# Values of a sparse attention on 64-column stationary tiles, in a fused attention and maxout kernel

## The chip, the cores and the metric

The kernel runs on one core of one Trainium2 chip. The metric is device time of one execution in microseconds (us). A core has TensorE for matmuls (PE in the profile; its weight loads have a row of their own, PEld), VectorE (DVE), ScalarE (ACT), GpSimd (POOL) and SyncE (SP), which issues most DMAs. A matmul takes a stationary operand (`lhsT`, loaded by an instruction of its own, LDWEIGHTS) and a moving one (`rhs`, streamed through), contracts over the partitions and writes into PSUM, on as many rows as `lhsT` has columns.

## The reference

Attention over q, k, v of shape 4 x 8 x 768 x 64 in fp32, then a maxout layer on the 3072 x 512 result. Each query sees the keys nearer than 16 positions, and 24 block summaries (block of 32: the maximum of the keys, the mean of the values), whose scores are raised by log 32:

```python
k_sum = k.reshape(B, H, nb, block, D).max(axis=3)
v_sum = v.reshape(B, H, nb, block, D).mean(axis=3)
scores_l = scale * np.matmul(q, k.transpose(0, 1, 3, 2))
mask_l = np.abs(pos[:, None] - pos[None, :]) < window
scores_s = scale * np.einsum('bhsd,bhnd->bhsn', q, k_sum) + np.log(block)
scores_all = np.concatenate([np.where(mask_l, scores_l, -1e9), scores_s], axis=-1)
a = softmax(scores_all)                       # over local keys and summaries
attn = np.matmul(a, np.concatenate([v, v_sum], axis=2))
x = attn.transpose(0, 2, 1, 3).reshape(B * S, H * D)
out = np.maximum(x @ w1, x @ w2) @ w_out
```

## The kernel before

**Tiling.** Queries go in 12 tiles of 64 per head. For each tile 128 rows of keys suffice: its neighbourhood and the 24 summaries, which lie among them in rows that the neighbourhood leaves free. So the scores of a query tile are one matmul of 128 keys by 64 queries (`scores`, L566). Two heads go together: head dimension 64 is the contraction, so the two heads' matmuls use rows 0 to 63 and 64 to 127 of the array, as pairs. ScalarE takes the exponential (L591) into tiles `pba` (the first eight query tiles) and `pbb` (the last four), VectorE masks them (L598; in the first batch a matmul adds the mask instead). A `pb` tile has shape 128 x 8 (or 4) x 192: for each head of the pair and each two query tiles it holds 64 columns of the even tile, 64 columns of zeros, and 64 columns of the odd tile. The zeros are set once at the start (`fixed_parts`), and exponential and mask write around them.

**Values.** `values` (L601 to L647) takes one batch, two head pairs (four heads) and one of three groups of four query tiles, 24 calls in all. Each call issues 16 matmuls (`mm`, L609 to L616) into two PSUM banks, one bank per head pair: for each pair of query tiles the even one has stationary columns 0 to 127 of the 192 (even tile, zeros) and the odd one columns 64 to 191 (zeros, odd tile). The moving operand is the values of that tile's 128 key rows with a column of ones (65 columns). The two accumulate, so that the even tile's results end on PSUM rows 0 to 63 and the odd one's on rows 64 to 127. Then VectorE takes the reciprocal of the sums (L625) and multiplies (L627) over all 128 rows, and the result x is transposed, by DMA (L632) or by TensorE (L640).

**Maxout.** x goes through the layer in groups of 256 tokens: w2 - w1 (`wd`) and a product w1 @ w_out (`w1o`, L707) are made once, so that the output is x @ w1o + relu(x @ wd) @ w_out: `hidden` (L723), relu on ScalarE (L728), and the output in `out_part` (L744, L751), copied out of PSUM at L456.

**Order.** A planner (`Plan.run`) sets the order of every engine when the program is made: each operation has an engine, an estimated time and a priority; the planner steps through time, starts on each engine the first ready operation of highest priority, keeps PSUM banks and SBUF buffers in rings, and then issues everything in the order found. The estimate for `values` is 0.48 us. On the chip each engine takes its instructions in that order, with semaphores between engines. Forty small matmul pairs on zeros (`idle`, L785) fill TensorE at the start. The first batch's attention comes early; the other batches' attention lies between the maxout work of the batch before, and the last 29 us are maxout alone.

Of the kernel before, what the change touches and what calls it, by code (L numbers as in the profile page):

```python
# [80 lines left out]
class Task:  # L81
    done, start = 1e9, None
# [29 lines left out]
class Plan:  # L112
# [9 lines left out]
    def op(self, engine, us, fn, read=(), write=(), change=(), touch=(), behind=(), prio=0.0, label="", port=False):  # L122
        t = Task()
        t.engine, t.us, t.fn, t.label = engine, us, fn, label
        t.port = engine == "POOL" or port and engine == "DVE"
        t.prio = (prio + CFG["bump"].get(label, 0), len(self.tasks))
        t.new, t.behind = [*write, *change], behind
        t.deps = {w for b in (*read, *change) for w in b.writers}
        for b in t.new:
            b.writers.append(t)  # L130
        for b in (*read, *touch, *t.new):
            b.users.append(t)
        self.tasks.append(t)
        return t
# [57 lines left out]
def kernel(  # L192
# [14 lines left out]
    nc = tc.nc  # L207
# [23 lines left out]
    def bank(buf, n=512, dt=F32):  # L231
        a = bank_tile[:, buf.slot:buf.slot + buf.width].rearrange("p b n -> p (b n)")
        return (a if dt is F32 else a.bitcast(BF16))[:, 0:n]
# [217 lines left out]
    def copy(engine, us, aps, label, port=True, **kw):  # L451
        engine = ENG[engine]
        us = us if isinstance(us, float) else us[engine[0]]
        def fn():
            o, i = aps()
            {"DVE": nc.vector.tensor_copy, "ACT": nc.scalar.copy,  # L456
             "POOL": nc.gpsimd.tensor_copy}[engine](out=o, in_=i)
        op(engine, us, fn, label=label, port=port, **kw)
# [142 lines left out]
    def values(b, hp, grp, pbs, prio, xt_on="D"):  # L601

        ps, tag = Buf(banks, "av", 2), f"{b}{hp}{grp}"

        def av(h=slice(0, 2)):
            return bank(ps, 1024).rearrange("p (h c) -> p h c", h=2)[:, h, 0:4 * (D + 1)].rearrange(
                "p h (n d) -> p h n d", d=D + 1)

        def mm(h):  # L609
            for n in range(4):  # L610
                u, a = n // 2, n % 2
                pairs = pbs[h][1].ap[:, 2 * a + u] if grp == 2 else pbs[h][0].ap[:, 4 * a + 2 * grp + u]
                for par in range(2):
                    nc.tensor.matmul(out=av()[:, h, n, :], lhsT=pairs[:, 64 * par:64 * par + 128],  # L614
                                     rhs=vx[b].ap[:, 4 * grp + 2 * u + par, 2 * (hp + h) + a, 0:D + 1],
                                     start=(par == 0), stop=(par == 1))  # L616

        op("PE", 0.48, lambda: [mm(h) for h in range(2)], read=[*(p[grp // 2] for p in pbs), ready[b, hp], ready[b, hp + 1]],
           touch=[vx[b]], write=[ps], prio=prio, label=f"values {tag}")
        turned = b > 0 and CFG["xd"][6 * b - 6 + 3 * (hp // 2) + grp] == "D"  # L620
        inv, x, xp = Buf(invr), Buf(xsr), None if turned else Buf(banks, "x")
        if hp == 0:
            xt[b, grp] = Buf(xtr)
        x_t = xt[b, grp]
        op("DVE", 0.18, lambda: nc.vector.reciprocal(out=inv.ap[:], in_=av()[:, :, :, D:D + 1]),  # L625
           read=[ps], write=[inv], prio=prio, label=f"inv {tag}")
        op("DVE", 0.69, lambda: nc.vector.tensor_tensor(  # L627
            out=x.ap[:], in0=av()[:, :, :, 0:D], in1=inv.ap[:].to_broadcast([128, 2, 4, D]), op=ALU.mult),
           read=[ps, inv], write=[x], prio=prio, label=f"x {tag}")

        if turned:
            op("SP", CFG["tus"][2], lambda: nc.sync.dma_start(  # L632
                out=x_t.ap[:, hp:hp + 2, :].rearrange("p h (u r) -> p (h u) r", r=128),
                in_=x.ap[:].rearrange("p h n d -> p (h n d)"), transpose=True),
               read=[x], write=[x_t], prio=prio, label=f"turn x{tag}")
            return

        def turn():
            for n in range(4):
                nc.tensor.transpose(out=bank(xp, 512, BF16)[:, 128 * n:128 * n + 128],  # L640
                                    in_=x.ap[:, n // 2, 2 * (n % 2):2 * (n % 2) + 2].rearrange("p a d -> p (a d)"),
                                    identity=identity[:])

        op("PE", 0.23, turn, read=[x], write=[xp], prio=prio, label=f"turn x{tag}")
        copy(xt_on, {"D": 0.42, "A": 0.62}, lambda: (
            x_t.ap[:, hp:hp + 2, :].rearrange("p h n -> p (h n)"), bank(xp, 512, BF16)), read=[xp], write=[x_t],
             prio=prio, port=False, label=f"xt {tag}")  # L647
# [209 lines left out]
```

## Time and profile before

| | |
|---|---|
| median of 3 runs | 173.47 us (172.87 to 174.89) |
| profiled execution, time | 174.2 us |
| profiled execution, span from first to last instruction | 172.5 us |
| granted TensorE clock | 1.00 |
| values, L614 | 256 matmuls from `pba`, 128 from `pbb` |
| L614 after 46.1 us | 288 matmuls |
| TensorE busy from 46.1 to 143.2 us | 97.09 of 97.10 us |

The page gives busy times by engine, the span in 40 slices (a digit is a busy share in tenths), the chain of work that ended last, and groups of instructions by source line, operand names and shape. In a shape such as `64*128 64x64`, the first part is the rows and columns of the array that the instruction uses and the second the partitions and elements of the operand it reads. In the chain in order of time a line has start, length, engine, tile, source line and the number of instructions merged. Matmuls overlap in their pipeline: one is recorded with its whole passage (193 ns for 65 columns), while the starts of two in a row are nearer together, and it is the starts that tell the pace.

### The profile page before, as it was taken

Reading aid. Unit: us, or ns where it says so; the run is one execution under the profiler, and the core shown is the slowest. Engines: PE = TensorE matmul, PEld = TensorE weight load, DVE = VectorE, ACT = ScalarE, POOL = GpSimd, SP = SyncE. Lnnn points to the kernel's source line nnn. Section 1 sums busy time; section 2 is a strip of 40 time slices with the busy share of each in tenths; the row PEclk is TensorE's granted clock in tenths of the full one; section 3 lists DMA queues with packets and bytes.
Section 4 is the critical chain, followed back from the end, with each engine's and each line's share of the span. In section 5 each row is a group of like instructions: output and inputs, shape, how many; then the busy total and the mean of one; then the engine's idle time right before and its main releaser. Section 6 shows DMA issues by size and latency. Waiting matters only on the chain.

```text
span 172.5 us, 4501 instructions
## 1 busy us (share of the span) xinstructions
PE 161.6 (94%) x1841; PEld 111.1 (64%) x1841; DVE 104.5 (61%) x220; ACT 93.7 (54%) x146; POOL 42.8 (25%) x73
## 2 busy tenths in 40 slices
PE   4886898999799999999999999999999999999992
PEld 4765667997355565577475776764747768756662
DVE  6799998997469994757985655939228360000001
ACT  3676873787661747363186484671665706524420
POOL 7725898032035070027201103101302000000000
PEclk9999999999999999999999999999999999999999
DMA  5999999999899999996599999967596516011113
GB/s 178 312 321 272 304 391 380 314 290 348 236 303 208 269 333 284 182 177 176 109 218 287 271 251 199 244 162 74 102 239 152 134 34 182 2 61 65 61 61 122
DMA packets 68980, 35.82 MB, mean 208 GB/s; under 512 B 56544, under 2 KB 62944, under 8 KB 68960
## 3 DMA queue, kind: packets, MB, share of 16 engines
q1 hardware_dynamic: 68816, 35.41, 83.6%
q8 instruction: 14, 0.23, 0.6%
q10 hardware_dynamic: 144, 0.13, 0.2%
q14 instruction: 6, 0.05, 0.1%
HBM read 25.17 MB, written 6.29 MB: 182 GB/s over the span
## 4 chain that ended last, share of the span: by engine, by line
PE 71%; DMA 14%; SPq 10%; DVE 1%; ACT 1%; issue 1%; DVEq 0%
PE banks L751 24%; PE banks L723 19%; PE banks L744 12%; DMA wf<-in_moe_w_dram 8%; DMA wf<-in_moe_w_out_dram 7%; PE banks L614 5%; SPq L366 4%; PE banks L566 3%; SPq L372 3%; PE banks L707 3%; SPq L659 3%; PE banks L421 2%; PE banks L509 2%; DVE wd L666 1%; PE banks L640 1%; ACT wo L456 1%
## 5 line engine op out<-in xcount | busy, mean ns | idle before, releaser
L751 PE MATMUL banks<-wo,g 128*128 128x512 bf16 (+2 forms) x208 | 46.7, 363 | 0.0
L723 PE MATMUL banks<-xt,wd 128*128 128x256 bf16 x384 | 46.4, 273 | 0.0
L723 PEld LDWEIGHTS <-wd 128*128 128x128 bf16 x384 | 36.8, 98 | 6.5
L728 ACT ACTIVATE g<-banks 128x512 bf16<-128x512 f32 x48 | 28.6, 598 | 16.8 <-PE banks L723 16.8
L456 ACT COPY o<-banks 128x512 f32<-128x512 f32 (+1 forms) x24 | 13.8, 576 | 34.9 <-PE banks L751 21.8
L751 PEld LDWEIGHTS <-g 128*128 128x128 bf16 x208 | 18.6, 97 | 17.3
L744 PE MATMUL banks<-w1o,xt 128*128 128x512 bf16 (+2 forms) x104 | 23.7, 363 | 0.0
L456 POOL CAST kqb<-kqf 128x768 bf16<-128x768 f32 x12 | 10.9, 908 | 40.8 <-PE banks L509 12.9
L591 ACT ACTIVATE pba<-banks 128x1024 bf16<-128x1024 f32 x16 | 16.4, 1023 | 5.3 <-PE banks L566 5.3
L456 DVE COPY o<-banks 128x128 f32<-128x128 f32 x2 | 0.6, 292 | 26.6 <-PE banks L751 26.6
L528 DVE TENSOR_REDUCE ks<-kx 128x24 bf16<-128x768 bf16 x16 | 14.9, 943 | 3.0 <-DMA kx<-kqb 2.8
L627 DVE TENSOR_TENSOR xs<-banks,inv 128x512 bf16<-128x512 f32 x24 | 16.3, 687 | 0.6
L598 DVE TENSOR_TENSOR pba<-pba,mask 128x1024 bf16<-128x1024 bf16 x12 | 8.3, 690 | 13.6 <-ACT pba L591 13.6
L744 PEld LDWEIGHTS <-xt 128*128 128x128 bf16 x104 | 9.8, 98 | 8.8
L456 POOL CAST vx<-vf 128x768 bf16<-128x768 f32 x7 | 7.3, 1040 | 23.1 <-DMA vf<-in_v_dram 23.0
L566 PEld LDWEIGHTS <-kx 64*128 64x128 bf16 x416 | 7.2, 95 | 6.7 <-issue 6.1
L456 POOL COPY kx<-kx 128x32 bf16<-128x32 bf16 (+1 forms) x12 | 6.0, 496 | 17.9 <-DMA kx<-kqb 11.4
L456 ACT CAST kqb<-kqf 128x768 bf16<-128x768 f32 x9 | 7.9, 881 | 4.5 <-DMA kqf<-in_k_dram 3.4
L785 PE MATMUL banks<-zeros 128*128 128x128 bf16 x80 | 8.4, 260 | 1.8 <-DVE zeros L781 1.8
L456 DVE COPY vx<-vx 64x3168 bf16<-64x3168 bf16 (+5 forms) x15 | 9.9, 677 | 0.2
L614 PEld LDWEIGHTS <-pba 128*128 128x128 bf16 x256 | 8.9, 97 | 1.5
L591 ACT ACTIVATE pbb<-banks 128x512 bf16<-128x512 f32 x16 | 9.5, 596 | 0.1
(82 smaller groups left out, 198.6 us busy)
## 6 DMA issues: line engine op xcount, KB each, us to landing
kqf<-in_k_dram SPq DMA_DIRECT2D x16, 384.0 KB, 5.8
kqf<-in_q_dram SPq DMA_DIRECT2D x16, 384.0 KB, 5.9
vf<-in_v_dram SPq DMA_DIRECT2D x16, 384.0 KB, 6.2
out_dram<-o SPq DMA_DIRECT2D x19, 256.0 KB, 3.7
wf<-in_moe_w_dram SPq DMA_DIRECT2D x4, 1024.0 KB, 9.4
wf<-in_moe_w_out_dram SPq DMA_DIRECT2D x2, 1024.0 KB, 10.1
out_dram<-o SPq DMA_DIRECT2D x4, 224.0 KB, 2.5
vx<-sums SPq DMA_DIRECT2D x2, 198.0 KB, 3.6
```

The source lines that it names most:

```text
L456: {"DVE": nc.vector.tensor_copy, "ACT": nc.scalar.copy, "POOL": nc.gpsimd.tensor_copy}[engine](out=o, in_=i)
L528: op("DVE", 0.95, lambda: nc.vector.tensor_reduce(out=ks.ap[:], in_=free(kt(), 128, [256, NM], [192, 2], [32, 2], [1, 32]), axis=AX.X, op= ...
L566: nc.tensor.matmul(out=bank(ps[i], 1024)[:, 512 * a + at + n0:512 * a + at + n1], lhsT=kx[b, hp].ap[r, 128 * t + 128:128 * t + 256], rhs=q ...
L591: op("ACT", (1.03, 0.6)[i], lambda: nc.scalar.activation(out=pv(), in_=bank(ps, 1024).rearrange("p (a c) -> p a c", a=2)[:, :, 0:64 * n], ...
L598: op("DVE", (0.69, 0.43)[i], lambda: nc.vector.tensor_tensor(out=pv(), in0=pv(), in1=m, op=ALU.mult), read=[mask_in], change=[pb], prio=pr ...
L614: nc.tensor.matmul(out=av()[:, h, n, :], lhsT=pairs[:, 64 * par:64 * par + 128], rhs=vx[b].ap[:, 4 * grp + 2 * u + par, 2 * (hp + h) + a, ...
L627: op("DVE", 0.69, lambda: nc.vector.tensor_tensor(out=x.ap[:], in0=av()[:, :, :, 0:D], in1=inv.ap[:].to_broadcast([128, 2, 4, D]), op=ALU. ...
L723: nc.tensor.matmul(out=bank(ps)[:, 256 * s:256 * s + 256], lhsT=wd[n].ap[:, c, 128 * s:128 * s + 128], rhs=x.ap[:, c, :], start=(c == 0), ...
L728: op("ACT", 0.6, lambda n=n, ps=ps: nc.scalar.activation(out=g.ap[:, 2 * n:2 * n + 2, :].rearrange("p f n -> p (f n)"), in_=bank(ps), func ...
L744: nc.tensor.matmul(out=bank(ps, c1 - c0), lhsT=x.ap[:, c, sl], rhs=w1o[c].ap[:, cols], start=(c == 0), stop=False)
L751: nc.tensor.matmul(out=bank(ps, c1 - c0), lhsT=g.ap[:, f, sl], rhs=wo[f // 2].ap[:, f % 2, cols], start=False, stop=(f == FC - 1))
L785: nc.tensor.matmul(out=bank(ps, 128), lhsT=zeros[:], rhs=zeros[:], start=True, stop=True)
```

## The change

Only the matmuls of `values` change. The even tile's stationary operand is columns 0 to 63 of the 192, and the odd one's columns 128 to 191: 64 columns each, without the zeros. Their outputs are PSUM rows 0 to 63 and rows 64 to 127, in the same bank and columns as before, so the program names array tiles of 128 rows by 64 columns at column positions 0 and 64. Each matmul starts and ends its own sum. The number and order of instructions on every engine, the planner's estimate, the zero columns and the memsets that make them stay as they were.

```diff
                 for par in range(2):
-                    nc.tensor.matmul(out=av()[:, h, n, :], lhsT=pairs[:, 64 * par:64 * par + 128],
+                    nc.tensor.matmul(out=av()[64 * par:64 * par + 64, h, n, :], lhsT=pairs[:, 128 * par:128 * par + 64],
                                      rhs=vx[b].ap[:, 4 * grp + 2 * u + par, 2 * (hp + h) + a, 0:D + 1],
-                                     start=(par == 0), stop=(par == 1))
+                                     start=True, stop=True)
```

## The prediction

> **What bounds the kernel now.** I read the page first: engine totals, slices, chain by line.
>
> ```profile
> PE 161.6 (94%) x1841; PEld 111.1 (64%) x1841; DVE 104.5 (61%) x220; ACT 93.7 (54%) x146; POOL 42.8 (25%) x73
> ...
> PE   4886898999799999999999999999999999999992
> ...
> PEclk9999999999999999999999999999999999999999
> ...
> PE 71%; DMA 14%; SPq 10%; DVE 1%; ACT 1%; issue 1%; DVEq 0%
> ```
>
> TensorE is busy in 94% of the span, at full clock, and carries 71% of the chain. The chain in order of time tells where that begins:
>
> ```profile
> 33.09 11.90 DMA wf<-in_moe_w_out_dram
> 45.02 1.05 ACT wo L456
> 46.11 3.61 PE banks L707 x16
> ...
> 65.96 0.48 PE banks L614 x16
> 66.44 0.86 PE banks L751 x4
> 67.31 0.46 PE banks L566 x26
> 67.77 0.97 PE banks L751 x4
> ...
> 70.69 0.97 PE banks L614 x32
> 71.66 1.73 PE banks L751 x8
> ```
>
> Until 45 us the chain is loads of weights, then one ACT copy; from 46.1 us to the end it is TensorE alone. So there are two stages. Before 46.1 us TensorE has room: the list of waits shows L707 waiting 1.1 us for ACT's wo and 0.2 us for POOL's, together some 1.25 us of standstill right at 46.1 us. After it, I compared the start of every matmul with the start before it plus its columns at 0.417 ns each and 2.5 ns; that fits 512 columns (216 ns apart), 256 (109) and 128 (56; 0.417 is (216 - 56)/384). No gap is over 40 ns too long except on both sides of the scores (L566) and after one first fp32 weight load. What the values cost or save there goes into the end one for one.
>
> The values (L614) show three things. A run of 32 matmuls takes 0.97 us and one of 16 takes 0.48 to 0.49 us, so 30.3 ns each; the neighbours (L751, 0.86 us for four) are undisturbed; and no weight load shows, since each starts 2 ns after the matmul ahead of its own:
>
> ```profile
> L614 PEld LDWEIGHTS <-pba x256: 94/97/102, 20.5 to 139.1; 128*128 128x128 bf16 x128
> L614 PE MATMUL banks<-vx,pba x256: 190/193/204, 20.6 to 139.1; 128*128 128x65 bf16 x128
> ```
>
> **The change, part by part.** Counts stay: 384 matmuls with 384 weight loads, the same order on TensorE, the same instructions on VectorE, ScalarE, GpSimd and SyncE; the memsets of the zero columns stay too. No wait, DMA or queue is moved. What changes is the form: 64 stationary columns for 128, outputs on rows 0 to 63 and 64 to 127 in turn, and no accumulation of the second onto the first. (That flag costs nothing on any row I see: the accumulating and the starting matmuls of L614 are equally far apart.) The trace of before has no matmul with 64 stationary columns. Three prices are needed.
>
> *Changing the tiling.* The nearest row is the scores, 64 rows by 128 columns in pairs:
>
> ```profile
> L566 PEld LDWEIGHTS <-kx x416: 92/95/97, 8.9 to 135.4; 64*128 64x128 bf16 x139
> L566 PE MATMUL banks<-qx,kx x416: 165/190/201, 8.9 to 135.5; 64*128 64x64 bf16 x118, 64*128 64x16 bf16 x12, 64*128 64x48 bf16 x9
> ...
>   issue: 6.1, 18
> ```
>
> Ahead of them the weight load stands still without a releaser ("issue", 18 times). In starts: 311 ns after a 512-column matmul where 216 is normal, so 95 ns to enter; 98 ns after the last pair where 9 is normal (16 columns), so 90 to leave, and 10 more because the first weight load behind it is not hidden (226 for 216). Together 195 ns. The chain above agrees: 13 pairs at 29 ns would be 0.38 us and the piece has 0.46; the four matmuls behind it take 0.97 for 0.86; 0.19 in all. The ends are 0, if this tiling needs no emptying of the array, and 195 ns; I take 195, as both are changes of tiling.
>
> *One weight load of 64 columns.* Where a load is not hidden, the matmul behind it is recorded longer by it: the first score matmul has 201 for 190 ns, so a 128-column bf16 load takes some 11 ns; the first fp32 transpose behind a change of tiling has 327 for 273, so 128 fp32 columns take 54 ns. The page's group means (95 to 98 and 147 ns) differ by about the same. The bounds for 64 columns are 6 ns (half of the one) and 54 ns. I take 27, an estimate (half of the fp32 row), because bf16 loads of 128 columns are read as four strips of 32 in the trace's operands, which 64 columns need not be. The Trainium skill, "TensorEngine Tiling (Array Packing)", Restrictions and Gotchas, speaks against the change here: column tiling excludes the fast weight load. "TensorE: Matmul & The Clock Gate", LDWEIGHTS, has a load at columns/1.2 ns, 53 ns for 64; its 107 ns for 128 is twice the fp32 row's 54, so the trace is not with that figure. With 53 ns, loads that take turns would make the sum below some 10 us.
>
> *Streaming.* 65 columns through all 128 rows: 30.3 ns from start to start now. The score pairs overlap (starts 3 ns apart, a pair every 29 ns), but on different rows of the array and partitions of SBUF. No row shows two matmuls streaming through the same 128 rows, nor two loads into the same rows at once. The bounds are 15 and 30 ns each. I take 30, the row with the same 128 rows; 27 ns of loading then fits beside 30 of streaming.
>
> *Sum.* After 46.1 us there are 18 groups (288 of the 384 matmuls) in 12 runs: six of 32 matmuls and six of 16, at 62.0, 65.8, 70.5, 73.4, 95.0, 98.0, 106.5, 108.9, 130.1, 132.8, 138.2 and 140.9 us. None lies next to scores, so each pays both changes: 95 + 27 (first load, unhidden) + 90 + 10 = 222 ns. 12 x 0.222 = **2.7 us**. The six groups before 46.1 us cost at most 6 x 0.222 = 1.3 us and lie ahead of the 1.25 us standstill and another 1.6 us of gaps between 24 and 42 us, so nothing; without that cover it would be 1.3 us more. Behind the values VectorE (reciprocal, product) starts up to 0.2 us later; what waits for it is a transpose (L640) for which TensorE stood 0.2 us in all, so no charge. Profiled execution: span 172.5 + 2.7 = 175.2 and time 174.2 + 2.7 = 176.9; that execution lies 0.7 us over the median 173.47, so the forecast for the median is **176.1 us** (+1.5%).
>
> **The rivals.**
>
> *Half of it takes turns, the other half not* (my case's other face): streams overlap, but the two loads of a pair follow each other, 54 ns a pair. 16 matmuls: 8 x 54 + 222 = 0.65 us for 0.487; 32: 1.09 for 0.971. 6 x (0.17 + 0.11) = 1.7 us, median 175.2. With the sum above this is my case, 175.0 to 176.3; chance 0.40.
>
> *Loads are not hidden at all, and all is in turn:* 27 + 30 = 57 ns each. 16: 0.91 + 0.195 = 1.11; 32: 1.82 + 0.195 = 2.02. 6 x (0.62 + 1.05) = 10.0 us: 183.5; the early groups would add 6 x 0.62 = 3.7 against 2.85 us of cover, so up to 0.9 more. Against it: loads into all 128 rows are hidden under matmuls on all 128 rows in every L614 row above; for it: there the load replaces the whole array, and no row shows a part. The Trainium skill, "TensorE: Matmul & The Clock Gate", Part 3, The mechanism, lets a load overlap a running matmul only on other rows; by that rule this is the outcome. The trace contradicts it for the whole array. Chance 0.27.
>
> *The other side: both tiles run fully side by side.* Pairs every 30 ns, as the scores' 29. 16: 8 x 30 + 222 = 0.46 for 0.487; 32: 0.70 for 0.971. 6 x (0.025 + 0.27) = 1.8 us less: 171.7. At 35 ns a pair, if the load just fails to hide, it is 1.1 us less: 172.4. It decides at about 42 ns a pair (144 pairs x 42 + 12 x 222 ns is the 8.75 us that the runs take now); below that the change wins. For it speak the scores' pairs; against it that those share no rows. The Trainium skill, "TensorEngine Tiling (Array Packing)", Key Properties, has different tiles load and multiply in parallel; by that rule this is the outcome. No run so far shows it for column tiles. Were the change of tiling free as well, 12 x 0.195 = 2.3 us more would go: 169.4. Chance 0.28, of it 0.03 without the price of changing.
>
> *The change is not one for the array* (neither emptying nor overlap, loads hidden): 0 us, 173.5. The program does name 128x64 tiles at two positions. Chance 0.05.
>
> **How the numbers follow.** My case is the likeliest: 176.1. The range 171.6 to 184.0 goes from the side-by-side case to the unhidden loads with some leakage from the early stage; outside stay the free change of tiling and loads dearer than 27 ns. About 1% (1.7 us) is what a measurement can tell from no change here: under 171.7 lies about half of the side-by-side case, 0.15; within lie its rest (0.13), the no-effect case (0.05) and the low end of mine (0.08), 0.26; above, 0.59.
>
> **What would show it.** My case: L614 starts 27 to 30 ns apart, the start behind a run 90 ns late, the matmul ahead of a run followed 95 ns late, runs in the chain of some 0.6 and 1.1 us, neighbours at 0.97 instead of 0.86. Side by side: starts in pairs 3 to 5 ns apart, runs of 32 near 0.6 us. Unhidden: some 57 ns apart, runs of 1.0 and 1.9 us. I am wrong if two column tiles do stream at once, if a 64-column load costs far from 27 ns, or if the emptying differs from that of the scores.

## The result, and the profile after

The changed kernel takes 172.66 us (median of 20 executions, 171.43 to 174.40) where the kernel before takes 173.43 (20, 172.54 to 174.94). The ratio is 0.9941, 95% interval 0.9912 to 0.9969: 1.0 us faster, 0.5 to 1.5. The medians lie 0.8 us apart; the ratio leaves out the three longest executions of the changed kernel, over 174 us, of which the profiled one (174.2 us, span 172.5) is one. I had forecast 2.7 us slower. A second profile, from the run `again` below, has 171.5 and 169.8. What they share is the cost of the values, and where they differ is told after it.

The first profile's page, engine totals, clock and chain by engine:

```profile
PE 160.5 (93%) x1841; PEld 106.6 (62%) x1841; DVE 102.4 (59%) x220; ACT 93.9 (54%) x146; POOL 41.7 (24%) x73
...
PEclk9999999999999999999999999999999999999999
...
PE 63%; DMA 17%; SPq 14%; DVE 2%; issue 1%; ACT 1%; POOL 0%; DVEq 0%
```

TensorE's share of the chain has gone from 71% to 63%, and the DMAs and SyncE's queue have taken it over. The chain in order of time (start, length, engine, tile, line, instructions merged), in the same stretch as before:

```profile
61.01 0.63 PE banks L614 x32
61.64 0.97 PE banks L751 x4
...
64.57 0.37 PE banks L614 x16
64.94 0.97 PE banks L751 x4
```

A run of 32 value matmuls takes 0.63 us where it took 0.97, one of 16 takes 0.37 for 0.48, and the four matmuls behind either take 0.97 for 0.86. The listing of line L614 shows the new form, 64 columns of the array:

```profile
L614 PEld LDWEIGHTS <-pba x256: 106/109/114, 21.0 to 139.0; 128*64 128x64 bf16 x128
L614 PE MATMUL banks<-vx,pba x256: 190/195/218, 21.0 to 139.0; 128*64 128x65 bf16 x128
```

The starts tell how. Inside a run a matmul and its neighbour on the other tile start 3 to 4 ns apart, and pairs follow each other at 25 to 31 ns (49 and 33 behind the first two), 31.6 ns from pair to pair with the 3 to 4 inside: 15.8 ns a matmul for 30.3 before. Two matmuls of 65 columns at 0.417 ns, 27 ns each, would not fit into 31.6 ns one behind the other, so they overlap. A run starts 309 ns after the last 512-column matmul (216 is normal), so 93 to enter; the first two matmuls are recorded with 217 ns for 193, so a first load shows with 24 ns; the matmul behind starts 128 ns after the last value for 30, so 98 to leave, and the one after that 10 late. From its first start to the start of the matmul behind it a run of 32 takes 629 ns and one of 16 takes 376. A run of 32 thus holds TensorE 93 + 629 + 10 = 732 ns for 971, and one of 16 holds it 93 + 376 + 10 = 479 for 487. Over six runs of each that is 6 x (0.239 + 0.008) = 1.5 us less work.

Yet this execution has the span of the one before. The list of what TensorE waited for after 46 us shows it; before, that list had only the 1.1 us for ACT's wo at 46.1 us:

```profile
PE banks L614 <- DMA vx<-sums: 0.7, 1, 0.7
PE banks L566 <- issue: 0.5, 1, 0.5
PE banks L421 <- DVE vx L456: 0.4, 1, 0.4
PE banks L614 <- DVE pba L598: 0.4, 1, 0.4
```

By the starts, gaps of 0.53 us at 94.2, 0.58 at 116.3, 0.85 at 130.1 and 0.54 at 135.3 us, 2.5 us together. The chain names what was late ahead of the first three:

```profile
86.64 6.29 DMA kqf<-in_q_dram
92.95 0.56 DVE kqb L456
93.51 0.61 DVE pba L598
...
109.71 5.88 DMA vf<-in_v_dram
115.61 0.57 DVE vx L456
...
126.41 3.67 DMA vx<-sums
```

A load of q, one of v, and the spreading of the block means. The q load shows how it came about. SyncE issues it at 86.64 us, in the profile before at 86.55, although TensorE had begun the values after 46 us 1.1 us earlier (60.94 for 62.00); in `again`, where they begin at 60.85, it is issued at 85.25. It also takes 6.29 us here and 5.08 in both others. From the first values after 46 us to the end, the kernel before needs 110.47 us, this one 111.52; without the 2.5 us of gaps it would be 109.0, which is 110.47 less the 1.5.

### The profile page after: what moved, and what is told of

The parts are those of the page before. It is cut to its first block, busy times and chain, and to the rows that moved or that the text cites. A ratio compares the mean times of both kernels' runs of the same rounds, so it can differ in the third digit from the quotient of the medians.

```text
span 172.5 us, 4501 instructions
## 1 busy us (share of the span) xinstructions
PE 160.5 (93%) x1841; PEld 106.6 (62%) x1841; DVE 102.4 (59%) x220; ACT 93.9 (54%) x146; POOL 41.7 (24%) x73
## 3 DMA queue, kind: packets, MB, share of 16 engines
HBM read 25.17 MB, written 6.29 MB: 182 GB/s over the span
## 4 chain that ended last, share of the span: by engine, by line
PE 63%; DMA 17%; SPq 14%; DVE 2%; issue 1%; ACT 1%; POOL 0%; DVEq 0%
PE banks L723 20%; PE banks L751 19%; PE banks L744 8%; DMA wf<-in_moe_w_dram 6%; SPq L366 5%; PE banks L707 4%; PE banks L614 4%; DMA kqf<-in_q_dram 4%; DMA vf<-in_v_dram 3%; SPq L372 3%; PE banks L509 2%; PE banks L566 2%; DMA vx<-sums 2%; SPq L659 2%; PE banks L421 2%
## 5 line engine op out<-in xcount | busy, mean ns | idle before, releaser
L728 ACT ACTIVATE g<-banks 128x512 bf16<-128x512 f32 x48 | 28.6, 598 | 15.6 <-PE banks L723 15.5
L456 POOL CAST vx<-vf 128x768 bf16<-128x768 f32 x7 | 6.4, 917 | 25.0 <-DMA vf<-in_v_dram 24.9
L456 DVE CAST kqb<-kqf 128x768 bf16<-128x768 f32 x11 | 6.7, 637 | 6.2 <-DMA kqf<-in_k_dram 4.4
L456 POOL COPY kx<-kx 128x32 bf16<-128x32 bf16 (+1 forms) x12 | 4.9, 405 | 22.2 <-DMA kx<-kqb 16.0
L566 PE MATMUL banks<-qx,kx 64*128 64x64 bf16 (+2 forms) x416 | 9.4, 190 | 0.5 <-issue 0.5
```

Source lines behind the costliest of these rows:

```text
L456: {"DVE": nc.vector.tensor_copy, "ACT": nc.scalar.copy, "POOL": nc.gpsimd.tensor_copy}[engine](out=o, in_=i)
L566: nc.tensor.matmul(out=bank(ps[i], 1024)[:, 512 * a + at + n0:512 * a + at + n1], lhsT=kx[b, hp].ap[r, 128 * t + 128:128 * t + 256], rhs=q ...
L728: op("ACT", 0.6, lambda n=n, ps=ps: nc.scalar.activation(out=g.ap[:, 2 * n:2 * n + 2, :].rearrange("p f n -> p (f n)"), in_=bank(ps), func ...
```

## The experiments

Theory A: two column tiles work side by side, which saves TensorE 1.5 us, and what TensorE saves runs into transfers that are only just in time, so that a part is waited away. Theory B: nothing is given back in waits; the change is worth 1.0 us because column tiles cost more than the trace tells.

**`again`.** The changed kernel unaltered, for a second profile.

> The changed kernel once more, for a second profile. Theory A: from the first values after 46 us to the end it takes what the kernel before takes (110.5 us) less 1.5 us, plus TensorE's waits, which differ from one execution to the next: the waits account for the difference to 109.0 us within 0.3 us. Time 171.5 to 173.5.

173.24 us (10 executions), ratio 0.9965 (0.9925 to 1.0005); the interval overlaps that of the 20. Its profile has a span of 169.8 us. TensorE's waits after 46 us:

```profile
PE banks L751 <- issue: 0.8, 5, 0.2
PE banks L707 <- issue: 0.2, 1, 0.2
PE banks L744 <- issue: 0.2, 1, 0.2
```

All seven "issue" waits of 0.2 us are places where the record of one 512-column matmul is missing (1822 of 1841 are there); no wait for data is left. From the first values to the end it is 108.9 us, 1.6 less than before, against 1.5 by the sum. The standstill at 46.1 us, 1.25 us in the profile before, is absent here as in the first profile; that makes the rest, 1.1 us, of the 2.7 us between the spans. It is no effect of the change that I can show: run `in_turn` has it again, 1.2 us long. So the same kernel ends at 169.8 or 172.5 us of span, depending on which transfers come in time. Theory A's account holds within 0.1 us in both profiles.

The times of `again` hold a second thing that neither theory has. Six of its ten executions have a mean granted clock of 0.99 and take 173.2 to 174.6 us; the four with 1.00 take 171.5 to 173.0. Two later profiles with 0.99, of `store_after` and `sums_dve`, show such an execution: the clock is half for 3.4 us, from 28.5 and 29.4 us on, and TensorE has stood for 1.4 us, up to 28.6 us, for a load of w. `in_turn` and `turn_pe` stand there for 1.6 us and keep the full clock. The first 20 executions of the changed kernel have no 0.99, the 31 of the kernel before that `again` is compared with have three. Whether the change makes this more frequent no run shows; it is a likely reason why `again` gives 0.6 us where the first 20 give 1.0.

**`store_before` and `store_after`.** Both kernels with 4 MB less to store, to take the transfers out of the way.

```diff
+            m = n if b == B - 1 else 16
...
-            queue.dma_start(out=out[b * S + at:b * S + at + n, cols], in_=o.ap[0:n, cols])
+            queue.dma_start(out=out[b * S + at:b * S + at + m, cols], in_=o.ap[0:m, cols])
```

> The kernel before, with the stores of batches 0 to 2 cut to 16 of 128 rows (their output is left out; the wrapped rows are still stored), so that the DMA engines have some 4 MB less to move between 46 and 143 us. Theory A (the changed kernel saves 1.5 us of TensorE after 46 us, and waits for loads take part of it back): this kernel falls by 0 to 2 us, by what TensorE waited before 46 us. Theory B (no give-back; the column tiles cost more than the trace shows): the same here; it serves as the partner of the next kernel.

> The changed kernel with the same cut of the stores (batches 0 to 2 store 16 of 128 rows). Theory A: against the kernel before with the same cut it is 1.3 to 1.7 us faster, more than the 0.8 to 1.0 us between the uncut kernels, and TensorE's waits after 46 us, 2.6 us in the profile of the changed kernel, are below 1 us. Theory B: the difference stays 0.8 to 1.0 us.

With the cut the kernel before takes 173.36 us (ratio to the uncut 0.9974, 0.9944 to 1.0004) and the changed one 171.44 (0.9871, 0.9835 to 0.9906). One against the other is 0.9897, or 1.8 us, and with both intervals added in squares 1.0 to 2.6. That includes theory A's 1.3 to 1.7 and touches theory B's 1.0, so the times alone don't decide. The profile does: in `store_after` no wait for data is left after 46 us, and from the first values to the end it takes 108.88 us, against 110.44 in `store_before`: 1.56 us, the whole sum. `again` came without waits too, with all its stores; so the pair shows that the sum arrives where nothing is late, and not that the stores are what makes the loads late.

**`half`.** Take away three times as much from TensorE, without column tiles: the odd query tiles are left out, and the zeros beside the even ones are ones, so that all sums stay finite.

```diff
-                for par in range(2):
-                    nc.tensor.matmul(out=av()[:, h, n, :], lhsT=pairs[:, 64 * par:64 * par + 128],
-                                     rhs=vx[b].ap[:, 4 * grp + 2 * u + par, 2 * (hp + h) + a, 0:D + 1],
-                                     start=(par == 0), stop=(par == 1))
+                nc.tensor.matmul(out=av()[:, h, n, :], lhsT=pairs[:, 0:128],
+                                 rhs=vx[b].ap[:, 4 * grp + 2 * u, 2 * (hp + h) + a, 0:D + 1],
+                                 start=True, stop=True)
```

> The kernel before with only the even matmul of each pair (128 stationary columns, of which the 64 zeros are ones here so that sums stay finite; odd query tiles are left out): half the streaming, no change of tiling. TensorE's work after 46 us falls by 18 x 0.244 = 4.4 us, three times what the changed kernel saves. Theory A (what is saved beyond some 1 us is waited away for loads): waits of TensorE after 46 us of 1.5 us or more, and 170 to 171.5 us. Theory B (no give-back): no such waits, 169.0.

171.62 us, ratio 0.9881 (0.9828 to 0.9935): 2.1 us less of the 4.4 that TensorE was spared, 0.1 us above theory A's range. Its waits after 46 us:

```profile
PE banks L566 <- POOL kx L456: 2.0, 1, 2.0
PE banks L421 <- DVE vx L456: 0.3, 1, 0.3
```

The 2.0 us are the scores of the last batch, whose keys come by a transposing DMA, as the chain of this run shows:

```profile
126.71 4.54 DMA kx<-kqb
...
131.37 0.53 POOLq L851
131.89 0.78 issue
132.67 0.53 PE banks L566 x25
```

By the starts the waits are 2.6 us, and without them the stretch from the first values is 106.2 us, 4.3 less than before; with them it is 108.8, so 1.6 of the 4.3 arrive there in this profile. No column tile is in this kernel, and about half of its saving is gone as well; theory B has nothing to say to that.

**`one_tile`.** Force what I had forecast: both query tiles on one array tile.

```diff
+        def fill(h):
+            nc.tensor.matmul(out=av()[:, h], lhsT=identity[:], rhs=vx[b].ap[:, 4 * grp, 0:4, 0:D + 1],
+                             start=True, stop=True)
...
-                    nc.tensor.matmul(out=av()[64 * par:64 * par + 64, h, n, :], lhsT=pairs[:, 128 * par:128 * par + 64],
+                    nc.tensor.matmul(out=av()[0:64, h, n, :], lhsT=pairs[:, 128 * par:128 * par + 64],
...
-        op("PE", 0.48, lambda: [mm(h) for h in range(2)], read=[*(p[grp // 2] for p in pbs), ready[b, hp], ready[b, hp + 1]],
+        op("PE", 0.48, lambda: [f(h) for f in (fill, mm) for h in range(2)], read=[*(p[grp // 2] for p in pbs), ready[b, hp], ready[b, hp + 1]],
```

> The changed kernel with even and odd query tiles both on the array tile of columns 0 to 63 (both write PSUM rows 0 to 63, the odd over the even; rows 64 to 127 get stand-in numbers from one identity matmul per bank ahead of the group, 260 columns, so the odd results are left out). It forces what my prediction assumed, streams one behind the other. To be read from the starts inside a run of 16. Theory A (the gain of the changed kernel is two tiles working at once): 29 to 33 ns apart, some 0.47 us from first to last start, for 0.25 in the changed kernel. Rival (the 64-column form itself is cheaper, whatever the tile): 0.25 us here too. Third (a load is hidden only behind the other tile): 25 + 30 ns, some 0.83 us.

In its chain, L618 is the values and L610 the stand-in matmuls:

```profile
66.92 0.23 PE banks L610 x2
67.14 0.62 PE banks L618 x16
67.77 0.97 PE banks L755 x4
```

0.62 us for 16 where two tiles take 0.37 (the whole kernel, with the stand-ins and their changes of tiling, took 182.8 us once). The starts lie 33 ns apart (496 ns from the first to the last), 16.5 with two tiles (248 ns). So the 64-column form is not cheaper in itself, rather a little dearer than 128 columns with their zeros (30.5, 457 ns); the gain is the second tile. The single matmuls here even follow each other as the pairs do with two tiles: at 0, 52, 88, 117 and 147 ns, there at 0, 53, 88, 118 and 152. Loads are hidden here too: 25 + 30 ns is not what the starts show.

**`in_turn`.** Four even tiles, then four odd ones, in each bank.

```diff
-            for n in range(4):
+            for par in range(2):
+                for n in range(4):
```

> The changed kernel with, in each bank, the four even tiles first and then the four odd ones, where they alternate. Theory A (two column tiles stream side by side, and neighbours in the queue must be of different tiles for that, as matmuls start in order): matmuls of one tile start 28 to 32 ns apart, and only where the tile changes 3 to 5 ns; a group's 16 matmuls take 0.37 us from first to last start in place of 0.25, 18 groups 2.1 us more than the changed kernel, about 174.5. Rival (my prediction's step: streams go one behind the other whatever the order): no difference to the changed kernel.

Neither came as told. A run of 32 takes 530 ns from first to last start and one of 16 takes 275, for 501 and 248 when alternating: 27 to 29 ns more a run, 0.3 us in all and not 2.1. The time is 173.17 us, ratio 0.9957 (0.9924 to 0.9989), not to be told from the changed kernel, as the rival had it; its reason, streams one behind the other, doesn't hold by `one_tile`. Theory A's side remark, that neighbours must be of different tiles, was wrong. The first four matmuls of a run, all of the even tile, start at 0, 13, 52 and 66 ns, nearer together than 65 columns take on one tile (33 ns in `one_tile`). It looks as if starts were recorded at the entry to a tile, where matmuls can line up behind each other; no run here tests that.

**`split`.** The loads doubled, streaming as it was.

```diff
+                for c0, c1 in ((0, 33), (33, D + 1)):
...
-                    nc.tensor.matmul(out=av()[64 * par:64 * par + 64, h, n, :], lhsT=pairs[:, 128 * par:128 * par + 64],
+                        nc.tensor.matmul(out=av()[64 * par:64 * par + 64, h, n, c0:c1],
+                                         lhsT=pairs[:, 128 * par:128 * par + 64],
-                                     rhs=vx[b].ap[:, 4 * grp + 2 * u + par, 2 * (hp + h) + a, 0:D + 1],
+                                         rhs=vx[b].ap[:, 4 * grp + 2 * u + par, 2 * (hp + h) + a, c0:c1],
```

> The changed kernel with each matmul of 65 moving columns cut into one of 33 and one of 32 with the same stationary operand loaded again, so that loads double and streaming stays. If a 64-column load of some 25 ns sets the pace of a pair: pairs stay 27 to 31 ns apart, a group takes 16 such pairs, 0.45 us in place of 0.25, and 18 groups cost 3.6 us more than the changed kernel: 176. If the streaming sets it (33 columns: 16 ns): pairs are some 16 to 18 ns apart, a group stays at 0.26 us, and the time is that of the changed kernel.

```profile
66.63 1.12 PE banks L615 x64
...
70.68 0.61 PE banks L615 x32
```

A group's matmuls doubled and so did its time: pairs of 33 and 32 columns stay 31.5 ns apart (64 matmuls in 1009 ns), as pairs of 65 did. So streaming doesn't set the pace of a pair. Whether the loads do (24 ns where one shows) or the four instructions of a pair stays open: the score pairs, whose loads show with 11 ns, keep 29 ns as well, also with 48 columns. The time, 180.33 us (ratio 1.0384, 1.0337 to 1.0432), is further up than the 3.6 us expected. 6 x (0.496 + 0.241) = 4.4 us of it are the twelve runs; the rest lies before them, since the first values after 46 us start at 66.6 us for 60.9 in the changed kernel, and the granted clock is 0.93 over the first 46 us: half from 29.0 to 35.8 us, after TensorE had stood for 1.7 us up to 28.7.

**`each_switch`.** A change of tiling ahead of every matmul.

```diff
+                    rows, cols = (slice(64, 128), slice(128, 192)) if par else (slice(0, 128), slice(0, 128))
-                    nc.tensor.matmul(out=av()[64 * par:64 * par + 64, h, n, :], lhsT=pairs[:, 128 * par:128 * par + 64],
+                    nc.tensor.matmul(out=av()[rows, h, n, :], lhsT=pairs[:, cols],
```

> The even query tile with 128 stationary columns (its zeros make rows 64 to 127), then the odd one as a 64-column tile over rows 64 to 127: the tiling changes ahead of every matmul of the values, 16 times a group in place of 2. Theory A (a change of tiling costs some 95 ns whatever is in flight): a pair takes 30 + 93 + 128 = 250 ns, a group 2.0 us for 0.49 before; 18 groups cost 27 us and the six early ones some 6 more beyond their cover: 200 to 210. Rival (the price is the emptying of long matmuls, and small behind 65 columns): half of that, about 188.

At full clock the starts are 134 ns apart into the column tile and 150 back, 284 a pair; less twice 30 of streaming, 224 ns for the two changes, so the price is the same behind 65 columns as behind 512 (201 and a first load of 24). But the time is 236.1 us (231.7 and 240.6), beyond the range. The clock row of the profile of the longer execution shows why:

```profile
PE   4968999999999999999999999999999999999994
PEld 4755567779665555645757666675656764485654
...
PEclk9999555559999958955899999999998895589999
```

In ten of forty slices the granted clock is near half, mostly with TensorE marked busy throughout; there the same pair takes 360 ns. Half clock holds for 68 us in all, which costs 34 us at most; at full clock this execution would have taken 206 us or more, an estimate, so the range may have failed by the clock alone. The clock falls five times, at 22.7, 84.2, 101.2, 183.1 and 196.8 us, each time inside a run of values; the runs of 32 at 133.2 and 150.0 us keep it full.

**`join3`, `plan_040`, `sums_dve`, `turn_pe`.** Attempts at a version that beats both. `join3` issues three groups in one run and gives the values six PSUM banks for four; the others change one number or letter each of what the planner goes by.

```diff
+        JOIN = {0: (0, 1, 2)} if b else {0: (0,), 1: (1,), 2: (2,)}
...
+            op("PE", 0.22 + 0.25 * len(gs), lambda: [mm(vps[b, hp, g], g, h) for g in gs for h in range(2)],
```

> The changed kernel with the three groups of two head pairs issued as one run of 48 matmuls in batches 1 to 3 (six PSUM banks at once, the planner told 0.97 us for the three), so six runs after 46 us in place of twelve and half the changes of tiling. By TensorE's sum: a run takes 23 x 31.6 + 222 = 0.95 to 0.98 us for 1.46 before, 6 x 0.48 = 2.9 us less than before, 170.5. Theory A: waits for loads take about half of what goes beyond the changed kernel, 171 to 172.5. Rival: the run has to wait for all exponentials and six banks, and the order found is worse: 173 or more.

188.23 us, ratio 1.0782 (1.0717 to 1.0846): the rival. A run is as short as the sum had it (93 + 882 + 10 = 985 ns for 48 matmuls). But the runs come late, the first after 46 us at 70.7 us for 60.9, and what hangs on them comes later. That each needs every exponential and six banks is the likely reason, which I have not separated from the new order. TensorE's longest waits after 46 us:

```profile
PE banks L736 <- DMA xt<-xs: 4.1, 1, 4.1
PE banks L653 <- DVE xs L640: 2.5, 1, 2.5
PE banks L421 <- POOL vx L456: 1.8, 1, 1.8
```

On top of them the granted clock is half from 82.0 to 88.8 and from 153.7 to 160.5 us, 0.96 in the mean.

> The changed kernel with the spreading of the block means of the last batch done by VectorE in place of two DMAs (vx from sums, 198 KB each, which TensorE waited 0.7 us for in the profile of the changed kernel). The planner finds another order. Theory A: one of the four waits after 46 us goes, 0.5 to 0.9 us, so 171.5 to 172.2, unless VectorE's 2 us more of work delay something else. Rival: no gain, another load is late instead.

```diff
-    lsr="DDS",
+    lsr="DDD",
```

172.24 us, ratio 0.9931 (0.9894 to 0.9968). Not to be told from the changed kernel (0.9941 and 0.9965), though no wait for the sums is left in its profile (which has the stretch of half clock told of at `again`).

> The changed kernel, the planner told 0.40 us for a group of values in place of 0.48 (the runs measured 0.32 to 0.47 a group). The order changes on all engines from the early stage on; TensorE's sum stays. If the order found fits the chip better, up to 1 us less than the changed kernel; if the waits for loads set the end, as theory A has it, within 1 us of it, 171.7 to 173.7.

```diff
-        op("PE", 0.48, lambda: [mm(h) for h in range(2)], read=[*(p[grp // 2] for p in pbs), ready[b, hp], ready[b, hp + 1]],
+        op("PE", 0.40, lambda: [mm(h) for h in range(2)], read=[*(p[grp // 2] for p in pbs), ready[b, hp], ready[b, hp + 1]],
```

174.93 us, ratio 1.0058 (1.0020 to 1.0095): slower than both, outside what I had expected. With an estimate nearer to the chip the planner's other choices came out worse; its profile has a gap of 1.4 us at 144 us that the changed kernel lacks. Which choice it was I have not separated.

> The changed kernel with one transpose of x in batch 3 moved from DMA to TensorE (0.22 us there, 0.42 us of copying on VectorE or ScalarE), so that the DMA queue has one transpose of some 2.6 us less. Theory A: TensorE has 1.5 us to spare and loads are what is late, so 0 to 0.8 us faster than the changed kernel, 171.9 to 172.7. Rival: no room, 172.7 to 173.3.

```diff
-    xd="D...DD.DD.DDDDDDDD",
+    xd="D...DD.DD.DDD.DDDD",
```

173.18 us, ratio 0.9973 (0.9935 to 1.0011): the rival, no room. So none of the four is shown to beat the changed kernel.

## Why the prediction was wrong

**What bounds the kernel.** "What the values cost or save there goes into the end one for one" was right as to work and wrong as to a saving. `half` gives 4.3 us back on TensorE and 2.1 in time. That TensorE had no gap after 46.1 us showed that nothing was late, not by how much things were early; the DMA engines' mean busy share, 0.95 between 46.1 and 143.2 us, was a sign that I left out, though no measure (0.94 in `again`, without a wait). One reading there was loose too: an fp32 transpose of 128 columns takes 109 ns to the next start and not 56, so more gaps than I named are over 40 ns too long; the sum isn't touched, as the change leaves these transposes alone.

**The counts.** Right: 12 runs, 18 groups, none beside scores. The six early groups cost nothing, as I had it: w1o starts at 41.98 us for 41.94.

**Changing the tiling, 195 ns.** Right: 93 + 98 + 10 = 201, and 224 with a first load in `each_switch`.

**One load, 27 ns.** Right within 3: 24 show. The Trainium skill, "TensorEngine Tiling (Array Packing)", Restrictions and Gotchas, has column tiling without the fast load; 24 ns for 64 columns where 128 show with 11 agree with it. The 53 ns by the Trainium skill, "TensorE: Matmul & The Clock Gate", LDWEIGHTS, are not what the trace has.

**Streaming, 30 ns each: the step that failed.** I took "the row with the same 128 rows" and gave the overlap of the scores to their separate rows. Two column tiles stream through the same 128 rows at once: 15.8 ns each, near the lower of my two bounds. Forced onto one tile they take 33, so as a price for one tile the 30 was fair. What paces a pair is not its streaming, since 33 columns take as long as 65 (`split`); what does stays open. With 15.8 in place of 30.3 the sum turns from +2.7 to -1.5 us.

**The rivals.** *Side by side* is what happened, with 31.6 ns a pair between the 30 and the 35 that I had set, and 1.5 us between 1.8 and 1.1; the point from which it decides, 42 ns a pair, stands. That the change would be worth less than its sum, through the transfers, I had in none of the rivals. The rule of the Trainium skill that tiles load and multiply in parallel ("TensorEngine Tiling (Array Packing)", Key Properties) agrees with the trace, 31.6 ns a pair. *Loads not hidden* falls: in `one_tile` loads into the same rows and columns stay hidden, 33 ns a matmul. With it falls, for this kernel, the rule of the Trainium skill, "TensorE: Matmul & The Clock Gate", Part 3, The mechanism, that a load overlaps running matmuls only where the rows differ; the same section also names a background weight buffer as a second way, and I had left that out.

**The numbers.** 172.66 lies in the range of 171.6 to 184.0, on the other side of no change from my 176.1; it is inside only because I had let the range reach down to the side-by-side rival. I had 0.59 on slower by over 1%, and 0.26 on what came, within 1%. Between two bounds a factor of two apart I let one row decide by likeness of shape, although the change lived by that very factor; the sign should have been left more open.

## What to carry to other kernels

Two 64-column tiles over the same 128 rows double the pace of short matmuls here, 15.8 for 30.3 ns, and each stay in another tiling costs some 0.22 us: it pays from about 16 matmuls of this kind in a run (a pair saves 60.6 - 31.6 = 29 ns), so runs of 16 gave 8 ns and runs of 32 gave 239. A profile without waits says that the bounding engine is never starved, not that it may become faster: take a full DMA row as a warning (0.95 here), and take away more than the change would (as in `half`) to see how much of a saving arrives. Runs may be lengthened only if nothing has to wait for the longer run: joining three groups made the kernel 13.6 us slower than the one before, where TensorE's sum had promised 2.9 us less.

## What the runs showed of the hardware

- Matmuls for one column tile may start 13 ns apart, and which tile comes next in the queue hardly matters: 27 to 29 ns a run between alternating and four by four (`in_turn`).
- A pair of column-tile matmuls follows the last after 31.5 ns whether it streams 65 columns or 33 (`split`), and on one tile alone single matmuls follow each other in 33 ns (`one_tile`).
- With a change of tiling ahead of every matmul of the values the granted clock was 0.855 over the whole of `each_switch`, though its TensorE row shows 96% busy; it fell to half five times, always inside a run of values. That the changes of tiling bring it down is likely from that and not tested apart.
- After TensorE had stood for 1.4 us the granted clock was half for 3.4 us in two profiles (`store_after`, `sums_dve`); after 1.6 us it stayed full in two others (`in_turn`, `turn_pe`).
